# Scatters of the first static block earlier, scaling of the second ahead of the next lists' sum, in a routed two-layer MLP behind pooled attention

## The chip, the cores and the metric

One core of one Trainium2 chip runs the whole program. The metric is device microseconds of one execution; lower is better. Engines are named as in the profile: PE is TensorE, DVE is VectorE, ACT is ScalarE, POOL is GpSimd, SP is SyncE (it only issues DMAs here).

## What is computed

Attention over pooled keys and values (8 batches, 8 heads, 576 positions, 72 pooled groups) gives 4608 rows of 512 numbers. Each row is routed to one of 8 experts, by the largest logit or, where a local gate says so, to the expert of the row before. The expert is a two-layer MLP with ReLU, and its result is scaled by the routing probability:

```python
for s in range(S):
    fresh_e = int(np.argmax(logits[b, s]))
    if s == 0 or local_gate[b, s] < 0.5:
        e = fresh_e
    else:
        e = prev_e if prev_e >= 0 else fresh_e
    prev_e = e
    ...
    h = np.maximum(x[b, s] @ w1[e], 0.0)
    out[b, s] = p[e] * (h @ w2[e])
```

## The kernel before

**Stages.** The first stage computes attention and routing for four pairs of batches and writes the rows to `x_rows` in DRAM. For each expert a list of its rows (row number and probability) is built in DRAM (`ids`) by POOL's scatters. The second stage works through the lists in blocks of 256 rows, two halves of 128. A block is: read its list entries, gather its rows by an indirect DMA from POOL, transpose them on PE, split them into a high and a low part (`x`), layer 1, layer 2, scale by the probability, scatter to `out` by an indirect DMA from POOL.

**One block on PE.** Layer 1 (`l1_mms`, L307 to L312) makes 8 slices of the hidden layer, each of 4 pairs of matmuls (L309 with 512 columns, L311 with 256) into a PSUM buffer `hp`. For each slice ACT copies a part out (L316), DVE adds the other (L317), ACT applies ReLU (L321) and DVE takes the low part (L322). From the second static block on, six PSUM buffers are in turn (three `hp`, two `tp`, one `rt`). Layer 2 (`l2`, L333) makes 24 matmuls for each half into `o_ps[h]`. Half 1 comes first, then the transposes of the rows of the next block (L277), then half 0.

**Static and dynamic blocks.** The first two blocks (numbered 0 and 1 here by "first and second static block") take the rows of the most frequent expert, and overlap with the end of attention; block number 2 (the "third block") is the first whose place in the lists comes from a table `tab` that DVE computes. It runs ahead of the loop as `two_halves` and `rest(1)`; all later ones run in a loop. `rest` scales and scatters the results of its block.

**Order.** In this stretch nothing is reordered by a scheduler: `PLAN`, `PLAN_B` and `PLAN_C` are lists of steps, carried out in that order by `do` (L731), and each engine gets its instructions in the order in which the steps issue them. An engine that waits holds all that it has behind. The steps around the change:

- `es:1`, `es:0` (L840): ACT scales the first static block's `o_ps` into `ob[:, h]`.
- `so:0`, `so:1` (L843): POOL scatters `ob[:, h]` to `out`, with row numbers `idr`. A scatter waits for the landing of the one before it.
- `fd.p:18`, `i1`, `g1` (L268): the last attention rows on POOL; list and gather (into `qt`) for the third block. `Y0`, `Y1`: its transposes and splits.
- `i2`, `i3` (L290): SP loads the list of the fourth and of the fifth block into the one tile `idp`, by 8 small DMAs each; `f1` (`ids_sum`, L297 and L294): DVE sums the four parts into `m_c` and converts the row numbers into `idk`. `i3` has to wait until `f1` has read `idp`.
- `f2` (L302): POOL gathers the fourth block's rows (into `vt_in`) by `idk`.
- `ma`, `f0`: DVE copies probabilities and row numbers of the second and third block to `m_a`, `m_i`, `m_b`.
- `M2:8` to `M2:15`: layer 2 of the second static block, half 0. Half 1 was done by `L2:16` to `L2:23`.
- `e1`: `emit_scale(1)` (DVE, L1046) scales the second static block's half 1 into `ob[:, 1]`, which the scatter `so:1` must have left; `emit_rows(1)` (POOL, L1055 to L1057) scatters it. At L1138 to L1140 the same for half 0, with `seen_o(1)` (POOL, L1049) between, which waits until the scatter of half 1 has landed.
- `ld:0`: SP loads the first changed expert's weights (4 MB) into `raw`; the first block that changes expert reads them.

Of the kernel before, what the change touches and what calls it, by code (L numbers as in the profile page):

```python
# [93 lines left out]
rV:3 L2:0 s:0 rP:3 fd.p:19 h0:7 s:0 L1:8 s:0 p2.d:2 L2:1 h1:6 L1:9 L2:2 ct:0 L2:3 L2:4 L2:5 s:0 h1:7 p2.d:3 h0:8 h0:9  # L94
L2:6 L2:7 tc:0 cn:0 s:0 L2:8 L2:9 s:0 s:0 s:0 h1:8 L1:10 L2:10 L1:11 h1:9 s:0 tb:0 h0:10 L1:12 s:0 h0:11 s:0 s:0 L2:11
tb:0 h1:10 L2:12 s:0 L1:13 L2:13 s:0 tb:0 tb:0 tb:0 s:0 s:0 es:1 h0:12 L1:14 L2:14 tb:0 h1:11 L2:15 s:0 es:0 L1:15
fd.p:18 L2:16 tb:0 i1:0 L2:17 g1:0 h0:13 tb:0 L2:18 h1:12 h1:13 h0:14 L2:19 L2:20 h0:15 h1:14 L2:21 h1:15 L2:22 L2:23
Y0:0 i2:0 Y1:0 f1:0 ma:0 i3:0 f2:0 so:0 so:1 f0:0
""")
PLAN_C = plan("""  # L100
ld:0 M2:8 M2:9 M2:10 M2:11 e1:0 M2:12 M2:13 M2:14 M2:15
""")

@with_exitstack
def moe_attention(ctx: ExitStack, tc: tile.TileContext, q, q_st, k, v, v_st, w_gate, w1, w2, out):
# [231 lines left out]
    with ExitStack() as actx:  # L337
# [393 lines left out]
        def do(name, n):  # L731
# [5 lines left out]
            elif op == "lk":  # L737
                kg[n] = prep_k(n // 2, n % 2)
                step(kg[n])
            elif op == "lv":  # L740
                vg[n] = prep_v(n // 3, n % 3)
                step(vg[n])
            elif op == "lc":
                late_consts()
            elif op == "pf":
                prefill()
            elif op == "ci":
                fill()
            elif op == "cm":
                mask_consts()  # L750
            elif op == "cr":
                route_consts()
            elif op == "cz":
                nc.gpsimd.memset(kdz[n], 0.0)
            elif op == "wa":
                warm()
            elif op in ("kp", "kc"):
                step(kg[n])
            elif op == "vm":
                place_v(n // 3, n % 3)  # L760
            elif op in ("vp", "vt", "vc", "vl", "vd"):
                step(vg[n])
            elif op == "sc":
                sc[n] = scores(qT.pop(n), *units[n])
                step(sc[n])
            elif op in ("mx", "sb"):
                step(sc[n])
            elif op == "ex":
                att[n] = Attend(step(sc[n]), *units[n])
            elif op in ("T0", "T1", "T2"):  # L770
                tr2[n, op] = att[n].transpose(int(op[1]))
                step(tr2[n, op])
            elif op in ("T0c", "T1c", "T2c"):
                drain(tr2[n, op[0:2]])
            elif op in ("v0", "v1", "v2"):
                vl[n, op] = att[n].values(int(op[1]))
                step(vl[n, op])
            elif op in ("v0c", "v1c", "v2c"):
                drain(vl[n, op[0:2]])
            elif op == "fr":  # L780
                pr = units[n][0]
                if pr not in lgs:
                    lgs[pr] = ap2.tile([P, NC, GL], F32, name="lg")
                fr[n] = att[n].scale(lgs[pr])
                step(fr[n])
            elif op == "fs":
                drain(fr[n])
            elif op == "fp":
                rw[n] = att[n].rows()
                step(rw[n])  # L790
            elif op == "fd":
                drain(rw[n])
            elif op == "rA":
                fin[n] = finish(lgs[n], n)
                step(fin[n])
            elif op in RSTEPS:
                step(fin[n])
            elif op == "s":
                scatter()
            elif op == "ch":  # L800
                choose()
            elif op == "er":
                reg["e"] = number(est_i[0:1, 0:1], (EN.SP,), E - 1)
                reg["row"] = number(est_i[0:1, 1:2], (EN.SP,), (E - 1) * REG // 32)
                reg["next"] = number(est_i[0:1, 2:3], (EN.SP,), (E - 1) * REG // 32 + NS * TB)
            elif op == "w1":
                first1[n] = ld.tile([P, F], F32, name="kt", bufs=2)
                load1(first1.get, reg["e"], [n])
            elif op == "w2":
                first2[n] = ld.tile([P, 2, D], F32, name="vt_in", bufs=3)  # L810
                load2(lambda c: first2[c].rearrange("p k n -> p (k n)"), reg["e"], [n])
            elif op == "p1":
                split1(first1[n], n, nc.vector if arg else nc.gpsimd)
            elif op == "p2":
                split2(first2[n], n, nc.vector if arg else nc.gpsimd)
            elif op == "il":
                rows_load(bass.ds(reg["row"] + n * TB, TB) if n else bass.ds(reg["row"], TB), n)
            elif op == "ga":
                xgs[n] = ld.tile([P, 2, D], F32, name="qt", bufs=4)
                rows_gather(n, xgs[n], 4 * S)  # L820
            elif op in ("X0", "X1"):
                xtp[n, op] = rows_turn(int(op[1]), xgs[n])
            elif op in ("X0c", "X1c"):
                if n not in xts:
                    xts[n] = (sp if n else ld).tile([P, KD, 2, 2 * P], F32R, name="x2", bufs=1)
                rows_split(int(op[1]), xtp[n, op[0:2]], xts[n])
            elif op == "ma":
                rows_meta(m_a, NS - 1)
                nc.vector.tensor_copy(out=m_i, in_=idrs[NS - 1])
            elif op == "L1":  # L830
                l1_mms(hp[n % 3], n % KF, xts[n // KF])
            elif op == "h0":
                l1_h(hp[n % 3], n % KF)
            elif op == "h1":
                l1_l(n % KF)
            elif op == "L2":
                l2(1 - n % 16 // KF, [n % KF])
            elif op == "es":
                h = n % 2
                nc.scalar.activation(out=ob[:, h, :], in_=o_ps[h], func=AF.Copy, scale=idms[n // 2][:, h, 1:2])  # L840
            elif op == "so":
                h = n % 2
                nc.gpsimd.indirect_dma_start(out=outv, out_offset=bass.IndirectOffsetOnAxis(ap=idrs[n // 2][:, h:h + 1], axis=0),  # L843
                                             in_=ob[:, h, :], in_offset=None, bounds_check=NT - 1, oob_is_err=False)
            elif op == "M2":
                l2(1 - n // KF, [n % KF])
            elif op == "tc":
                table_consts()
            elif op == "tb":
                step(tg)  # L850
            elif op == "ct":
                acc = state["acc"]
                reg["ct"] = ps_t.tile([P, 512], F32, name="tp")
                nc.tensor.matmul(out=reg["ct"][:, 0:E], lhsT=ones, rhs=acc, start=True, stop=True)
            elif op == "cn":
                nc.vector.tensor_scalar(out=nots2, in0=isf, scalar1=done[:, 0:1], scalar2=None, op0=ALU.mult)
                nc.vector.tensor_tensor(out=cnt, in0=reg["ct"][:, 0:E], in1=nots2, op=ALU.subtract)
                nc.vector.scalar_tensor_tensor(out=cnt, in0=isf, scalar=float(2 * P + 1), in1=cnt, op0=ALU.mult, op1=ALU.max)
            elif op == "i1":
                rows_load(bass.ds(reg["next"], TB), NS)  # L860
            elif op == "g1":
                xgs["n"] = ld.tile([P, 2, D], F32, name="qt", bufs=4)
                rows_gather(NS, xgs["n"])
            elif op in ("Y0", "Y1"):
                xt = xts[NS - 1]
                xtp["n", op] = rows_turn(int(op[1]), xgs["n"])
                rows_split(int(op[1]), xtp["n", op], xt)
            elif op == "i2":
                ids_load(bass.ds(entry(2, 1, (EN.SP,), NU32 - TB), TB))
            elif op == "ld":  # L870
                n0 = entry(0, 3, (EN.SP,), E - 1)
                load1(rw1, n0)
                load2(rl2, n0)
            elif op == "e1":
                emit_scale(1)
                emit_rows(1)
            elif op == "f0":
                rows_meta(m_b, NS)
            elif op == "f1":
                ids_sum()  # L880
            elif op == "f2":
                xg = ld.tile([P, 2, D], F32, name="vt_in", bufs=3)
                gather()
            elif op == "i3":
                ids_load(bass.ds(entry(3, 1, (EN.SP,), NU32 - TB), TB))
            else:
                raise ValueError(name)
# [247 lines left out]
        l2(1)  # L1135
        turn_next()

    emit_scale(0)  # L1138
    seen_o(1)
    emit_rows(0)  # L1140
    hp += [ps_t.tile([P, 512], F32, name="tp") for _ in range(2)] + [ps_r.tile([P, 512], F32, name="rt")]
    two_halves()
    chg, nx = changes(1)
# [55 lines left out]
```

## Time and profile before

| | us |
|---|---|
| runs (3) | 648.17, 649.9, 650.04; median 649.9 |
| profiled execution | 654.89 |
| its span, first to last instruction | 653.2 |
| PE busy in it | 610.4 (93%) |
| DVE, ACT, POOL busy | 397.9, 289.6, 279.0 |
| mean granted clock of PE | 0.976 of full speed |

All durations below come from the profiled execution, which took 5.0 us more than the median of the runs. A timeline row gives the start, the duration of one (or of xN merged), the engine, the line, the operation with the tile that it writes and those that it reads (buffer numbers left out), and, in brackets, how long the engine was idle before it and what ended that. Starts are us from the first instruction. A matmul's row is longer than the step to the next one, since matmuls overlap.

### The profile page before, as it was taken

The page shows a single profiled execution, that of the slowest core. Times are in us where ns is not written, and L with a number is a line of the kernel's source. Part 1 is how long each engine was busy: PE and PEld are TensorE (multiplying, and loading weights), DVE is VectorE, ACT ScalarE, POOL GpSimd, SP SyncE. Part 2 cuts the span into 40 slices and gives each one's busy share as a digit, 9 for nine tenths or more (in the row PEclk, how much of TensorE's full clock was granted, in tenths as well). Part 3 has the DMA queues.
Part 4 walks back from the last instruction along what each step waited for, and adds up shares of the span by engine and source line. Part 5 has one row for each costly group of instructions (what it writes and reads, how often), then busy time and mean ns, then how long its engine had stood idle before and what let it go on. Part 6 is the DMA issues. An engine that isn't in the chain of part 4 may idle for free. (4 is left out here: it accounts for less than half of the span.)

```text
span 653.2 us, 14583 instructions
## 1 busy us (share of the span) xinstructions
PE 610.4 (93%) x3492; PEld 526.1 (81%) x3493; DVE 397.9 (61%) x964; ACT 289.6 (44%) x692; POOL 279.0 (43%) x480
## 2 busy tenths in 40 slices
PE   5999999989999499999999999999999996999991
PEld 4998988878877478888888888888888885888881
DVE  6998898898754143533672574778253578444350
ACT  3777767855422122331642363755132555233230
POOL 4896766854651233223043333335332155213312
PEclk9999999989999889999999999999999997999996
DMA  8998976834011742022272156457311077302101
GB/s 318 377 377 277 371 285 180 277 100 178 18 33 34 249 140 59 22 65 65 84 238 65 43 161 193 156 194 242 120 41 53 26 260 264 117 27 65 49 16 52
DMA packets 55112, 96.21 MB, mean 147 GB/s; under 512 B 30762, under 2 KB 30762, under 8 KB 55084
## 3 DMA queue, kind: packets, MB, share of 16 engines
q1 hardware_dynamic: 46572, 73.81, 33.8%
q0 software_dynamic: 8512, 22.07, 10.4%
q8 instruction: 13, 0.21, 0.1%
q14 instruction: 15, 0.12, 0.1%
HBM read 75.74 MB, written 22.21 MB: 150 GB/s over the span
## 5 line engine op out<-in xcount | busy, mean ns | idle before, releaser
L309 PE MATMUL hp<-x,w1h 128*128 128x512 f32 x364 | 135.2, 410 | 14.4 <-DVE hs L317 9.2
L333 PE MATMUL o_ps<-w2h,ht_h 128*128 128x512 f32 x312 | 124.0, 398 | 0.0
L333 PE MATMUL o_ps<-w2l,ht_h 128*128 128x512 f32 x312 | 122.1, 391 | 0.8 <-DVE w2l L176 0.7
L311 PE MATMUL hp<-x,w1l 128*128 128x256 f32 x364 | 103.9, 285 | 0.0
L309 PEld LDWEIGHTS hp<-x,w1h 128*128 128x128 f32 x364 | 70.6, 194 | 34.1 <-DVE hs L317 10.3
L333 PE MATMUL o_ps<-w2h,ht_l 128*128 128x512 f32 x312 | 87.6, 390 | 0.0
L316 ACT COPY hs<-hp 128x256 f32<-128x256 f32 x91 | 33.5, 370 | 119.6 <-PE hp L311 109.6
L321 ACT ACTIVATE ht_h<-hs 128x256 fp32r<-128x256 f32 x136 | 57.1, 420 | 40.1 <-DVE hs L317 29.0
L1046 DVE TENSOR_SCALAR ob<-o_ps,m_a 128x512 f32<-128x512 f32 x42 | 31.4, 750 | 67.8 <-PE o_ps L333 41.5
L311 PEld LDWEIGHTS hp<-x,w1l 128*128 128x128 f32 x364 | 70.9, 195 | 0.5
L333 PEld LDWEIGHTS o_ps<-w2l,ht_h 128*128 128x128 f32 x312 | 58.8, 188 | 12.4 <-DVE w2l L176 1.7
L333 PEld LDWEIGHTS o_ps<-w2h,ht_l 128*128 128x128 f32 x312 | 58.6, 188 | 12.5
L333 PEld LDWEIGHTS o_ps<-w2h,ht_h 128*128 128x128 f32 x312 | 58.8, 188 | 11.9
L538 PE MATMUL op<-vaug,aT 128*128 128x148 f32 (+4 forms) x448 | 65.6, 305 | 0.6 <-ACT osb L354 0.5
L317 DVE TENSOR_TENSOR hs<-hp,hs 128x256 f32<-128x256 f32 x91 | 37.6, 421 | 45.9 <-ACT hs L316 41.4
L1066 POOL TENSOR_TENSOR vt_in<-idk,zf 128x2 f32<-128x2 f32 x20 | 3.9, 195 | 143.1 <-PE tp L277 70.0
L538 PEld LDWEIGHTS op<-vaug,aT 128*128 128x128 f32 (+1 forms) x448 | 60.0, 178 | 3.9 <-issue 1.3
L322 DVE SCALAR_TENSOR_TENSOR ht_l<-hs,ht_h 128x256 fp32r<-128x256 f32 x136 | 56.6, 418 | 5.9 <-ACT ht_h L321 4.8
L1057 POOL DMA_INDIRECT out<-ob,m_e x42 | 47.9, 1142 | 20.9 <-issue 20.9
L302 POOL DMA_INDIRECT vt_in<-x_rows,idk x42 | 45.4, 1080 | 23.7 <-issue 12.9
L284 ACT CAST x<-tp 128x512 fp32r<-128x512 f32 x46 | 24.8, 587 | 55.7 <-PE tp L277 53.5
L1049 POOL TENSOR_TENSOR ob<-zf 128x1 f32<-128x1 f32 x41 | 9.1, 223 | 93.3 <-DMA out<-ob,m_e 83.3
(251 smaller groups left out, 1168.9 us busy)
## 6 DMA issues: line engine op xcount, KB each, us to landing
raw<-in_moe_w SPq DMA_DIRECT2D x56, 512.0 KB
kk<-in_k SPq DMA_DIRECT2D x16, 576.0 KB
qt<-in_q SPq DMA_DIRECT2D x16, 512.0 KB
vt_in<-in_v SPq DMA_DIRECT2D x16, 512.0 KB
x_rows<-xs SPq DMA_DIRECT2D x16, 512.0 KB
idp<-ids SPq DMA_DIRECT2D x176, 1.0 KB
vt_in<-in_v_st SPq DMA_DIRECT2D x8, 256.0 KB
vt_in<-in_moe_w SPq DMA_DIRECT2D x4, 512.0 KB
```

What stands on the lines that cost most here:

```text
L284: nc.scalar.copy(out=xt[:, cs, 0, :], in_=tv)
L302: nc.gpsimd.indirect_dma_start(out=xg[:, h, :], out_offset=None, in_=x_rows[0:NT + 1], in_offset=bass.IndirectOffsetOnAxis(ap=idk[:, h:h + ...
L309: nc.tensor.matmul(out=ps, lhsT=W1[0][:, kk, f * P:(f + 1) * P], rhs=xt[:, kk].rearrange("p i n -> p (i n)"), start=(kk == 0), stop=False, ...
L311: nc.tensor.matmul(out=ps[:, 0:2 * P], lhsT=W1[1][:, kk, f * P:(f + 1) * P], rhs=xt[:, kk, 0, :], start=False, stop=(kk == KD - 1), skip_g ...
L316: nc.scalar.copy(out=hb[:, 0, :], in_=ps[:, 2 * P:])
L317: nc.vector.tensor_tensor(out=hb[:, 1, :], in0=ps[:, 0:2 * P], in1=hb[:, 0, :], op=ALU.add)
L321: nc.scalar.activation(out=ht[0][:, f, :], in_=hb, func=AF.Relu)
L322: nc.vector.scalar_tensor_tensor(out=ht[1][:, f, :], in0=hb, scalar=0.0, in1=ht[0][:, f, :].bitcast(F32), op0=ALU.max, op1=ALU.subtract)
L333: nc.tensor.matmul(out=to[h], lhsT=ht[i][:, kk, h * P:(h + 1) * P], rhs=W2[j][:, kk, :], start=(n == 0), stop=(n == 3 * KF - 1))
L538: nc.tensor.matmul(out=out, lhsT=lhs, rhs=rhs if len(out.shape) == 3 else rhs.rearrange("p s x -> p (s x)"), start=all(x[0] != n for x in ...
L1046: nc.vector.tensor_scalar(out=ob[:, h, :], in0=o_ps[h], scalar1=m_a[:, h, 1:2], scalar2=None, op0=ALU.mult)
L1057: nc.gpsimd.indirect_dma_start(out=outv, out_offset=bass.IndirectOffsetOnAxis(ap=m_e[h][:, 0:1], axis=0), in_=ob[:, h, :], in_offset=None, ...
```

## The change

The scatters `so:1` and `so:0` move from the end of `PLAN_B` to ahead of the gather `g1`, half 1 first. The scaling and scatter of the second static block (`e1`, and a new step `e0` in place of L1138 to L1140) move ahead of `f1`, `i3` and `f2`, and with them the last matmuls of its layer 2 (`M2:8` to `M2:15`), which stand ahead of `e0`.

```diff
@@ PLAN_B, PLAN_C
-fd.p:18 L2:16 tb:0 i1:0 L2:17 g1:0 h0:13 tb:0 L2:18 h1:12 h1:13 h0:14 L2:19 L2:20 h0:15 h1:14 L2:21 h1:15 L2:22 L2:23
-Y0:0 i2:0 Y1:0 f1:0 ma:0 i3:0 f2:0 so:0 so:1 f0:0
+fd.p:18 so:1 L2:16 tb:0 i1:0 L2:17 so:0 g1:0 h0:13 tb:0 L2:18 h1:12 h1:13 h0:14 L2:19 L2:20 h0:15 h1:14 L2:21 h1:15 L2:22
+L2:23 Y0:0 i2:0 Y1:0 ma:0 f0:0 e1:0 M2:8 M2:9 M2:10 M2:11 M2:12 M2:13 M2:14 M2:15 e0:0 f1:0 i3:0 f2:0
 """)
 PLAN_C = plan("""
-ld:0 M2:8 M2:9 M2:10 M2:11 e1:0 M2:12 M2:13 M2:14 M2:15
+ld:0
 """)
@@ do
-            elif op == "e1":
-                emit_scale(1)
-                emit_rows(1)
+            elif op in ("e0", "e1"):
+                h = int(op[1])
+                emit_scale(h)
+                if not h:
+                    seen_o(1)
+                emit_rows(h)
@@ ahead of the loop
-    emit_scale(0)
-    seen_o(1)
-    emit_rows(0)
     hp += [ps_t.tile([P, 512], F32, name="tp") for _ in range(2)] + [ps_r.tile([P, 512], F32, name="rt")]
     two_halves()
```

In the changed kernel the lines behind `do`'s branch stand 3 higher in number (L1046 becomes L1049), and those behind the removed calls are back at their old numbers. The order of PE's, ACT's and SP's instructions is the same in both. On VectorE, from the split of the third block's rows (L285) to layer 1 of that block (L317), the order before was (`o_ps_2327` is half 1, `o_ps_2326` half 0):

```order
L285 TENSOR_TENSOR x_2488<-tp,x_2488 128x2x256 x2
L297 TENSOR_REDUCE m_c<-idp 128x4
L294 TENSOR_SCALAR idk<-m_c 128x2
L271 COPY m_a<-idm_129 128x4
L829 COPY m_i<-idr_132 128x2
L271 COPY m_b<-idm_130 128x4
L1046 TENSOR_SCALAR ob<-o_ps_2327,m_a 128x512
L1046 TENSOR_SCALAR ob<-o_ps_2326,m_a 128x512
L317 TENSOR_TENSOR hs<-hp_2323,hs 128x256
```

and now:

```order
L285 TENSOR_TENSOR x_2488<-tp,x_2488 128x2x256 x2
L271 COPY m_a<-idm_129 128x4
L829 COPY m_i<-idr_132 128x2
L271 COPY m_b<-idm_130 128x4
L1049 TENSOR_SCALAR ob<-o_ps_2327,m_a 128x512
L1049 TENSOR_SCALAR ob<-o_ps_2326,m_a 128x512
L297 TENSOR_REDUCE m_c<-idp 128x4
L294 TENSOR_SCALAR idk<-m_c 128x2
L317 TENSOR_TENSOR hs<-hp_2323,hs 128x256
```

The sum of the lists (L297, L294) has moved behind both scalings. On POOL, behind the last list scatter (L675), the order before was:

```order
L576 TENSOR_TENSOR xs<-osb,rr 128x512
L268 DMA qt<-x_rows,idr_133 128x512 x2
L302 DMA vt_in<-x_rows,idk 128x512 x2
L843 DMA out<-ob,idr_131 4608x512 x2
L1055 TENSOR_TENSOR m_e_2311<-m_i,zi 128x1
L1056 TENSOR_TENSOR zf_2316<-m_e_2311,ob 128x1
L1057 DMA out<-ob,m_e_2311 4608x512
L1049 TENSOR_TENSOR ob<-zf_2314 128x1
L1055 TENSOR_TENSOR m_e_2310<-m_i,zi 128x1
L1056 TENSOR_TENSOR zf_2316<-m_e_2310,ob 128x1
L1057 DMA out<-ob,m_e_2310 4608x512
```

and now:

```order
L576 TENSOR_TENSOR xs<-osb,rr 128x512
L843 DMA out<-ob,idr_131 4608x512 x2
L268 DMA qt<-x_rows,idr_133 128x512 x2
L1058 TENSOR_TENSOR m_e_2311<-m_i,zi 128x1
L1059 TENSOR_TENSOR zf_2316<-m_e_2311,ob 128x1
L1060 DMA out<-ob,m_e_2311 4608x512
L1052 TENSOR_TENSOR ob<-zf_2314 128x1
L1058 TENSOR_TENSOR m_e_2310<-m_i,zi 128x1
L1059 TENSOR_TENSOR zf_2316<-m_e_2310,ob 128x1
L1060 DMA out<-ob,m_e_2310 4608x512
L302 DMA vt_in<-x_rows,idk 128x512 x2
```

The two scatters of the first static block (L843) have moved ahead of the third block's gathers (L268), and the fourth block's gathers (L302) behind both scatters of the second static block.

## Rows read from the trace of the kernel before

**Rows 1.** The page, busy tenths in 40 slices of 16.3 us; PEclk is the granted clock.

```profile
PE   5999999989999499999999999999999996999991
...
PEclk9999999989999889999999999999999997999996
```

**Rows 2.** Waits, 185 to 245 us: waiter, releaser, us in total, times, longest.

```profile
DVE ob L1046 <- DMA out<-ob,idr: 13.4, 1, 13.4
...
PE hp L309 <- DVE hs L317: 9.2, 2, 8.5
```

**Rows 3.** Timeline of DVE (VectorE), 204 to 226 us.

```profile
204.81 1.29 DVE L285 TENSOR_TENSOR x<-tp,x 128x512 fp32r<-128x512 f32 x2 [2.99 <-ACT x L284]
211.18 0.18 DVE L297 TENSOR_REDUCE m_c<-idp 128x4 f32<-128x16 f32 x1 [5.08 <-DMA idp<-ids]
...
225.21 1.41 DVE L1046 TENSOR_SCALAR ob<-o_ps,m_a 128x512 f32<-128x512 f32 x2 [13.43 <-DMA out<-ob,idr]
```

**Rows 4.** Timeline of ACT (ScalarE), 191 to 196 us.

```profile
191.66 0.68 ACT L840 ACTIVATE ob<-o_ps,idm 128x512 f32<-128x512 f32 x1
...
195.14 0.69 ACT L840 ACTIVATE ob<-o_ps,idm 128x512 f32<-128x512 f32 x1 [2.23 <-PE o_ps L333]
```

**Rows 5.** Timeline of POOL (GpSimd), 198 to 228 us.

```profile
198.67 1.01 POOL L268 DMA_INDIRECT qt<-x_rows,idr  x1 [8.04 <-DVE idr L259]
...
211.83 0.94 POOL L302 DMA_INDIRECT vt_in<-x_rows,idk  x1 [10.76 <-DVE m_b L271]
...
214.34 1.03 POOL L843 DMA_INDIRECT out<-ob,idr  x1 [0.31 <-issue]
218.93 1.00 POOL L843 DMA_INDIRECT out<-ob,idr  x1 [3.57 <-DMA out<-ob,idr]
...
226.90 1.00 POOL L1057 DMA_INDIRECT out<-ob,m_e  x1 [0.61 <-issue]
```

**Rows 6.** Timeline of PE, 203 to 233 us: start, duration, operation, [idle before, releaser].

```profile
203.61 0.98 PE L277 MATMUL tp<-ident,qt 128*128 128x128 f32 x7 [0.56 <-DMA qt<-x_rows,idr]
...
209.90 0.39 PE L309 MATMUL hp<-x,w1h 128*128 128x512 f32 x1
...
218.25 0.28 PE L311 MATMUL rt<-x,w1l 128*128 128x256 f32 x1
227.00 0.80 PE L309 MATMUL hp<-x,w1h 128*128 128x512 f32 x1 [8.46 <-DVE hs L317]
...
232.29 0.54 PE L333 MATMUL o_ps<-w2h,ht_h 128*128 128x512 f32 x1
```

**Rows 7.** Windows: stretch, us, busy by engine (instructions), PEclk, DMA share, GB/s.

```profile
222.00:223.00 1.00, 0.00 (x0) 0.00 (x0) 0.00 (x0) 0.00 (x0) 0.00 (x0) 0.68 0.97 352
232.00:233.00 1.00, 1.00 (x5) 0.83 (x4) 0.17 (x2) 0.42 (x2) 0.00 (x0) 0.70 0.20 74
```

**Rows 8.** Line 1057, the scatters of the dynamic blocks: start of issue to landing.

```profile
DMA to landing us min/median/max: 2.3/2.8/7.4
```

**Rows 9.** Timeline of PE, a later block of 256 rows.

```profile
281.09 0.39 PE L309 MATMUL hp<-x,w1h 128*128 128x512 f32 x1
...
292.38 0.40 PE L333 MATMUL o_ps<-w2h,ht_h 128*128 128x512 f32 x1
...
304.22 0.39 PE L309 MATMUL hp<-x,w1h 128*128 128x512 f32 x1
```

**Rows 10.** Timeline of SP's queue, 203 to 221 us.

```profile
203.57 13.97 SPq L290 DMA_DIRECT2D idp<-ids  x16
218.76 1.96 SPq L163 DMA_DIRECT2D raw<-in_moe_w  x4
```

**Rows 11.** Line 170, first reads of the loaded weights: durations in ns, first and last start.

```profile
L170 ACT CAST w1h<-raw x24: 1037/1047/1053, 318.4 to 538.9; 128x1024 fp32r<-128x1024 f32 x24
```

**Rows 12.** Windows, columns as in group 7.

```profile
199.00:200.00 1.00, 1.00 (x6) 0.85 (x5) 1.00 (x9) 0.71 (x3) 0.70 (x2) 1.00 0.00 0
214.00:215.00 1.00, 1.00 (x7) 0.89 (x6) 0.00 (x0) 0.00 (x0) 0.69 (x2) 1.00 0.66 211
```

## The prediction

> **What bounds the kernel now.** I read the page's slices first [rows 1]: TensorE (PE) is at 9 tenths nearly everywhere, so time is to be had only where it dips. It dips to 4 in slice 14 (212 to 229 us), and the granted clock falls in slices 14 and 15. The longest waits of the stretch [rows 2] name the chain: VectorE (DVE) held its scaling of `ob` for 13.4 us until the DMA `out<-ob,idr` had landed, and PE's layer-1 matmul waited for VectorE's next sum in `hs`, 9.2 us in two waits. The timelines show it in order. VectorE reads the new lists at 211.18 (after 5.08 us of waiting for `idp`) and then starts nothing until 225.21, when both scalings run [rows 3]. They overwrite `ob`, which holds the first static block's rows; ScalarE had filled it by 192.34 and 195.83 [rows 4], yet POOL scatters these rows only at 214.34 and 218.93, behind four gathers, and the second scatter starts 3.57 us after the first, whose landing it waits for [rows 5]. PE fills its six result buffers and stops after 218.25; it resumes at 227.00, 8.46 us idle [rows 6]. The clock of PE passes from its 2.4 GHz level to 1.2 GHz within 222 to 223 and returns within 232 to 233 [rows 7], so the last two of the eight slices run at half speed.
>
> **What the change does, and the sum.** It adds and removes no computation; it moves POOL and VectorE steps.
>
> *The two scatters, to ahead of the gather for the third block.* The VectorE wait that they ended was 13.4 us [rows 2]. Now the first can be issued right after 192.34. An issue takes 1.03 us [rows 5], and such a scatter lands 2.3 to 2.8 us after its start in the shortest and median case, 7.4 in the longest [rows 8]. So the first lands about 195.2; the second needs ScalarE's 195.83 as well, starts about 196.0, ends its issue about 197.1 and lands by 198.8. At 206.1, when VectorE has split the last rows [rows 3], `ob` is free: that wait goes whole.
>
> *What it is worth is read from PE, not from VectorE's 13.4 us.* Layer 1 of an undisturbed block, the same 64 matmuls in the same shapes, takes 292.38 − 281.09 = 11.29 us [rows 9]. Begun at 209.90 it ends at 221.19, where in the trace it ends at 232.29 [rows 6]: **11.10 us**, 8.46 of waiting and 2.6 of half clock. Layer 2 of this block ran at the high clock from 233 on; I count nothing there. The Trainium skill, "TensorE: Matmul & The Clock Gate" (Part 1, What's actually happening), puts the ramp penalty at under 1% of a typical span for modelling and advises against fitting a count of slow matmuls: by that the sum would leave the 2.6 us out and end near 641.4. The trace agrees with the size (0.4%), but it is a quarter of this gain, so the rows' sum counts it.
>
> *The scalings, to ahead of the lists' sum.* The first needs layer 2's first half, done before 203; it runs about 206.4 to 207.1. The second needs PE's last matmul before 209.90 plus its drain, and ends about 210.9. The lists come in at 211.18 as before, so their sum is not later. The queue behind it on VectorE is the sum of slice 0, which can't start before about 211.9 anyway. Cover: PE has six slices of buffers and stops only at 218.25, so lists up to 6 us late would cost nothing. I cost this at 0; without that cover it would cost each microsecond in full.
>
> *The gather for the third block, now behind the scatters on POOL.* Before, it started at 198.67, when VectorE had its row numbers [rows 5]; the second scatter's issue ends 197.1, so 0 is my value. PE already waits 0.56 us for this gather [rows 6], so any delay counts in full. Upper bound: both scatters take 7.4 us; the second starts at 200.4, the gather at 201.7, 3.0 us late. A gain here is excluded: row numbers and rows come when they did. I take 0.1, nearest to the median landing.
>
> *The next gather (`vt_in`), now behind two scatters of the second block.* A scatter starts 0.94 us after its scaling (225.96 to 226.90) [rows 3, 5], so about 208.1; POOL waits for its landing (210.9 in the median case), issues the second at about 211.9 and the gathers at 213.2 and 214.5, against 211.83 before. They land about 217.3. PE transposes them after layer 1 and half of layer 2: 221.19 + 5.5 = 226.7 (half of 304.22 − 292.38, less the transposes) [rows 9]. Worst case, every landing 7.4 us: 208.1 + 7.4 + 0.9 + 1.3 + 1.3 + 7.4 = 226.4. Still in time: 0 to 0.5, I take 0.
>
> *SP's queue is passed by nothing, but its waits are.* Its second set of list loads waits for the sum on VectorE; that stays at 211.4, so the loads of the next expert start at 218.76 as before [rows 10]. Nobody reads them until 318.4 [rows 11], 88 us of cover after the last is issued. After this block everything is PE's own sequence, at 9 tenths to the end but for one stall that hangs on its own block (slice 34) [rows 1], so the gain arrives at the end.
>
> Sum: −11.10 + 0.1 = −11.0 us. The profiled execution took 654.89 us (span 653.2), which would become 643.9; it is 5.0 us above the median of the runs, 649.9, so on the runs I forecast 649.9 − 11.0 = **638.9 us**.
>
> **The rivals.**
> *A. The wait moves to the third block's gather.* The scatters stand ahead of it, in the stretch in which VectorE is densest (199 to 200: busy 1.00 [rows 12]), and land late. For it: POOL waits in order, and PE already waits for this gather. Against it: the gather's issue at 198.67 took 1.01 us under that VectorE load, the scatter's at 214.34 1.03 us with VectorE idle [rows 5, 12], so issuing isn't slowed there; and DMA is idle at 199 [rows 12]. Price by the bound above up to 3.0 us: 640 to 642. The Trainium skill, "SBUF — State Buffer" (SBUF: two separate sides, with its part on the bandwidth-pool intuition), says that a VectorE operation in a two-port mode locks GpSimd out and starves the descriptors of its DMAs; it gives some 620 ns alone against 3100 ns beside a copy, by which I estimate 2.5 us more for each scatter. That would put the time at about 642; the two issues above speak against it.
>
> *B. No change.* VectorE would have to stay blocked. The second scaling waits for the second scatter; for the old stall it would have to land after 225. Even at 7.4 us each it lands at 207.8, before PE's result at 210 lets the scaling run. Time 649.9.
>
> *C. Slower: the gather into `vt_in` meets the weight loads.* It now leaves nearer to 218.76, and the hardware queue then carries 4 MB. If it stood behind all of them (the clock row of 232 to 233 shows DMA share falling to 0.20 there [rows 7]) and took 7.4 us more, it would land at 239.4: PE would wait 12.7 us at 226.7 and lose 2.6 to the clock again, 15.3 against 11.1 gained: 654.1 us. It decides from a landing after about 235.2; the longest landing in the trace would have to be nearly three times as long. For it: the longest landings are those under loads, and the scatter issued at 218.93 held VectorE until 225.21. Against it: its issue ends over 3 us before the loads begin.
>
> **How the numbers follow.** Forecast 0.85, A 0.08, B 0.03, C 0.04. A measurement of this kernel can tell about 0.3%, 2 us. Forecast and A are faster by more: 0.93; B is the same: 0.03; C slower: 0.04. The range goes from the lowest run less the full gain, 648.17 − 11.3 = 636.9, rounded to 636.5, to A's bound of 641.9 with the runs' scatter, 642.5.
>
> **What would show it.** PE's layer 1 of the second static block without idle time and at clock 1.00, ending near 221.2; the scatters `out<-ob,idr` on POOL at about 192.7 and 196.0; the scaling rows of VectorE at about 206.4 and 210.1, the second ended by PE and not by a DMA; `qt` gathered at 198.7 and PE's wait for it still about 0.6 us; `vt_in` gathered near 213.2 with no wait of PE at its transposes. The prediction is wrong if PE idles over a microsecond anywhere between 203 and 235, if the clock falls there, or if the end moves by less than the second block does.

## The result, and the profile after

| | before | changed |
|---|---|---|
| median of the runs beside each other, us | 649.75 | 640.06 |
| runs, us | 648.17 to 650.04 (4) | 638.51 to 641.49 (4) |
| ratio of the runs, 95% interval | | 0.9855 [0.9826, 0.9885] |
| profiled execution, us (its span) | 654.89 (653.2) | 639.39 (637.5) |
| mean granted clock | 0.976 | 0.984 |

By the ratio the changed kernel is faster by 9.4 us (7.5 to 11.3 by the interval; the two medians differ by 9.7), and its median lies in the predicted range of 636.5 to 642.5. The same kernel, run twice more beside the experiments, gave 0.9821 [0.9799, 0.9843] in one group and 0.9847 [0.9822, 0.9871] in the other. The forecast, 638.9 of 649.9, is a ratio of 0.9831 and lies in all three.

The slices of the page, PE's busy tenths and granted clock. PE's 4 in slice 14 and the clock's 8s in slices 14 and 15 [rows 1] are gone:

```profile
PE   5999999989999999999999999999999987999991
...
PEclk9899999999999999999999999999999997999996
```

The two profiles differ by 15.5 us, more than the runs do. So I compare stretches, not totals. PE in the changed kernel (start, duration, operation, [idle before, releaser]):

```profile
198.13 1.07 PE L277 MATMUL tp<-ident,qt 128*128 128x128 f32 x5
...
204.84 0.39 PE L309 MATMUL hp<-x,w1h 128*128 128x512 f32 x1
...
216.13 0.40 PE L333 MATMUL o_ps<-w2h,ht_h 128*128 128x512 f32 x1
...
229.09 0.47 PE L933 MATMUL hp<-w1h,x 128*128 128x512 f32 x1 [0.97 <-DVEq L1148]
```

Layer 1 of the second static block now takes 216.13 − 204.84 = 11.29 us without an idle row, where it took 22.39 [rows 6]. It begins 5.07 us earlier than before. Of that, 0.42 us are the eight transposes of the third block's rows, which took 1.15 us after 1.57; the rest was there before them. I don't put it down to the change: over the ten profiles of this study the time from the first transposes of routed rows (about 150 us) to this layer is 55.5 to 58.2 us in the five with the scatters ahead of the third block's gather, and 55.2 to 58.3 us in the five with them behind it. From the start of this layer to layer 1 of the next 256-row block, half block included, it was 257.89 − 209.90 = 47.99 us and is now 241.86 − 204.84 = 37.02: **10.97 us gained here**. At the start of that layer PE is 16.0 us ahead of its old times, and from there to the end it stays 15.6 to 16.2 us ahead, so about 0.4 us of it is lost later.

VectorE in the changed kernel, the rows that answer to [rows 3]:

```profile
201.16 0.74 DVE L1049 TENSOR_SCALAR ob<-o_ps,m_a 128x512 f32<-128x512 f32 x1
205.04 0.75 DVE L1049 TENSOR_SCALAR ob<-o_ps,m_a 128x512 f32<-128x512 f32 x1 [3.14 <-PE o_ps L333]
205.90 0.18 DVE L297 TENSOR_REDUCE m_c<-idp 128x4 f32<-128x16 f32 x1
```

Neither scaling waits for a landing any more; the second waits for PE, and the lists' sum behind it finds `idp` there already. POOL, the rows that answer to [rows 5]:

```profile
187.46 1.02 POOL L843 DMA_INDIRECT out<-ob,idr  x1 [0.17 <-issue]
192.43 0.99 POOL L843 DMA_INDIRECT out<-ob,idr  x1 [3.95 <-ACT hs L316]
193.73 0.98 POOL L268 DMA_INDIRECT qt<-x_rows,idr  x1 [0.30 <-DVE rowf L1036]
...
202.88 1.02 POOL L1060 DMA_INDIRECT out<-ob,m_e  x1 [0.65 <-issue]
205.81 0.18 POOL L1052 TENSOR_TENSOR ob<-zf 128x1 f32<-128x1 f32 x1 [1.91 <-DMA out<-ob,m_e]
...
206.97 1.02 POOL L1060 DMA_INDIRECT out<-ob,m_e  x1 [0.57 <-issue]
208.30 1.00 POOL L302 DMA_INDIRECT vt_in<-x_rows,idk  x1 [0.30 <-issue]
```

All four scatters are issued by 208, before SP issues the weight loads at 213.14. PE's granted clock is 1.00 over the whole of 195 to 240 us. The window in which it fell before [rows 7], which in this profile lies at the half block's transposes, now reads (us, busy by engine, clock, DMA share, GB/s):

```profile
222.00:223.00 1.00, 1.00 (x10) 0.91 (x8) 0.70 (x2) 0.73 (x2) 0.20 (x1) 1.00 1.11 447
```

### The profile page after: what moved, and what is told of

The parts are those of the page before. It is cut to its first block, busy times and chain, and to the rows that moved or that the text cites. A ratio compares the mean times of both kernels' runs of the same rounds, so it can differ in the third digit from the quotient of the medians.

```text
span 637.5 us, 14589 instructions
## 1 busy us (share of the span) xinstructions
PE 606.4 (95%) x3492; PEld 524.5 (82%) x3493; DVE 398.5 (63%) x964; ACT 289.9 (45%) x692; POOL 278.4 (44%) x480
## 5 line engine op out<-in xcount | busy, mean ns | idle before, releaser
L309 PE MATMUL hp<-x,w1h 128*128 128x512 f32 x364 | 133.0, 405 | 5.4 <-DVE x L285 5.2
L333 PEld LDWEIGHTS o_ps<-w2l,ht_h 128*128 128x128 f32 x312 | 58.7, 188 | 10.8
L1049 DVE TENSOR_SCALAR ob<-o_ps,m_a 128x512 f32<-128x512 f32 x42 | 31.5, 749 | 56.9 <-PE o_ps L333 52.6
L317 DVE TENSOR_TENSOR hs<-hp,hs 128x256 f32<-128x256 f32 x91 | 37.8, 421 | 46.3 <-ACT hs L316 45.1
L302 POOL DMA_INDIRECT vt_in<-x_rows,idk x42 | 45.4, 1081 | 13.1 <-issue 9.9
L284 ACT CAST x<-tp 128x512 fp32r<-128x512 f32 x46 | 24.8, 587 | 55.5 <-PE tp L277 53.3
```

The lines of the kernel that those rows point to most:

```text
L284: nc.scalar.copy(out=xt[:, cs, 0, :], in_=tv)
L302: nc.gpsimd.indirect_dma_start(out=xg[:, h, :], out_offset=None, in_=x_rows[0:NT + 1], in_offset=bass.IndirectOffsetOnAxis(ap=idk[:, h:h + ...
L309: nc.tensor.matmul(out=ps, lhsT=W1[0][:, kk, f * P:(f + 1) * P], rhs=xt[:, kk].rearrange("p i n -> p (i n)"), start=(kk == 0), stop=False, ...
L317: nc.vector.tensor_tensor(out=hb[:, 1, :], in0=ps[:, 0:2 * P], in1=hb[:, 0, :], op=ALU.add)
L333: nc.tensor.matmul(out=to[h], lhsT=ht[i][:, kk, h * P:(h + 1) * P], rhs=W2[j][:, kk, :], start=(n == 0), stop=(n == 3 * KF - 1))
L1049: nc.vector.tensor_scalar(out=ob[:, h, :], in0=o_ps[h], scalar1=m_a[:, h, 1:2], scalar2=None, op0=ALU.mult)
```

## The experiments

Eight runs, of six further kernels and of the change twice, in two groups on one chip. In the first group, of four, the kernel before took 650.11 us, in the second 654.48; so each run is compared with the kernel before of its own group. "L1 to L1" is the stretch named above, from layer 1 of the second static block to layer 1 of the next 256-row block: 47.99 us before, 37.02 in the change.

### Which half of the change does it?

The kernel before with the two scatters moved, and nothing else:

```diff
-fd.p:18 L2:16 tb:0 i1:0 L2:17 g1:0 h0:13 ...
+fd.p:18 so:1 L2:16 tb:0 i1:0 L2:17 so:0 g1:0 h0:13 ...
-Y0:0 i2:0 Y1:0 f1:0 ma:0 i3:0 f2:0 so:0 so:1 f0:0
+Y0:0 i2:0 Y1:0 f1:0 ma:0 i3:0 f2:0 f0:0
```

> The change's first part alone: the two scatters of the first static block ahead of the third block's gather; the lists' sum stays ahead of the scalings. Theory (the wait for the scatters' landing was the whole loss, the order of sum and scalings is worth nothing): VectorE reads the lists at about 211, scales right after until about 213, PE has no idle time in layer 1 of the second static block, and the ratio to before is that of the change, 0.983 to 0.986. Rival (the scalings' move brings a share of its own): VectorE or PE still waits at least 2 us there, ratio 0.989 or more.

Measured: 638.63 us, ratio 0.9836 [0.9811, 0.9861]; layer 1 in 219.20 − 207.91 = 11.29 us, L1 to L1 37.20. The change, run beside it:

> The change itself, unaltered, timed against before in five rounds. Theory (11.0 us in the second static block, nothing else): ratio 0.983 (0.981 to 0.985), and layer 1 of the second static block takes 11.3 us on PE in this profile too. Rival (the change costs something elsewhere, or the profile's earlier start of that block belongs to it): ratio 0.985 or more with 11.3 us in layer 1, or a start of the block near 205 us again where before has 210.

Measured: 638.5 us, ratio 0.9821 [0.9799, 0.9843], layer 1 in 11.29 us, L1 to L1 37.10. One sign named for the rival did come: the block starts at 203.77 us. But it starts at 203.94 in a kernel below whose scatters stand behind the third block's gather, so an early start doesn't come with the change. The two intervals overlap, and the stretch of 37.20 us lies within 0.2 us of the change's (37.02, 37.10, and 37.20 in its third profile): the scatters carry the whole gain, and the earlier scaling adds nothing that can be measured. VectorE of the kernel with the scatters alone:

```profile
208.63 0.18 DVE L297 TENSOR_REDUCE m_c<-idp 128x4 f32<-128x16 f32 x1 [4.54 <-DMA idp<-ids]
...
209.14 1.40 DVE L1046 TENSOR_SCALAR ob<-o_ps,m_a 128x512 f32<-128x512 f32 x2
```

The scalings still stand behind the lists, and are done at 210.5, soon enough for slice 0. What the earlier scaling buys is slack on POOL, as that queue shows in the same kernel:

```profile
217.40 1.01 POOL L1057 DMA_INDIRECT out<-ob,m_e  x1 [0.57 <-issue]
225.45 0.18 POOL L1049 TENSOR_TENSOR ob<-zf 128x1 f32<-128x1 f32 x1 [7.03 <-DMA out<-ob,m_e]
225.83 0.20 POOL L1066 TENSOR_TENSOR vt_in<-idk,zf 128x2 f32<-128x2 f32 x1 [0.20 <-PE tp L277]
```

Here the block's last scatter is issued after SP has begun the weight loads (215.87) and seen landed 8.05 us after its start; POOL is just in time for the next fetch, which PE's transposes release at 225.6. In the changed kernel's first profile POOL has seen that landing at 210.59 and then waits for PE:

```profile
210.59 0.20 POOL L1052 TENSOR_TENSOR ob<-zf 128x1 f32<-128x1 f32 x1
222.75 0.20 POOL L1069 TENSOR_TENSOR vt_in<-idk,zf 128x2 f32<-128x2 f32 x1 [11.96 <-PE tp L277]
```

### Ahead of which gather must the scatters stand?

The kernel before with the scatters moved past one gather only (`f2`), still behind the one for the third block (`g1`):

```diff
-Y0:0 i2:0 Y1:0 f1:0 ma:0 i3:0 f2:0 so:0 so:1 f0:0
+Y0:0 i2:0 Y1:0 f1:0 ma:0 i3:0 so:0 so:1 f2:0 f0:0
```

> Before, but with the two scatters moved only past the fourth block's gather (vt_in), which waits for the lists; they stay behind the third block's gather (qt). Theory (the loss came from standing behind a gather that waits for lists): the scatters start at about 201.4 and 204.5, land by 208.8, VectorE scales from 211.8 on without a wait for them, ratio as the change, 0.983 to 0.986. Rival (they must stand ahead of the third block's gather to land in time): VectorE waits for them past 214 and PE loses at least 2 us, ratio 0.988 or more. Should placing them ahead of the third block's gather cost anything, this one is faster than the change.

Measured: 639.48 us, ratio 0.9845 [0.9825, 0.9866]; layer 1 in 11.29 us, L1 to L1 37.57. The scatters start 8.5 us ahead of layer 1, as said, and 3.2 us ahead of it, 2.2 us later than said, since the first takes longer to land; VectorE has no wait for either. POOL:

```profile
195.44 1.03 POOL L843 DMA_INDIRECT out<-ob,idr  x1 [0.30 <-ACT ht_h L321]
200.73 1.00 POOL L843 DMA_INDIRECT out<-ob,idr  x1 [4.26 <-DMA out<-ob,idr]
206.22 0.99 POOL L302 DMA_INDIRECT vt_in<-x_rows,idk  x1 [4.49 <-DVE m_b L271]
```

POOL waits for the lists at the third row, as it did before, for 10.76 us [rows 5]; only now the scatters have left ahead of that wait. Two steps swapped in a list give the gain of the whole change, as far as the intervals tell; L1 to L1 is 0.4 to 0.6 us longer than in the change's profiles. The loss of the kernel before was that ready scatters stood behind a gather that couldn't start.

### Is it the buffer, or the landing?

The kernel before, its scatters late as they were, but with the first static block's rows in a buffer of their own, so that VectorE has no landing to wait for:

```diff
-nc.scalar.activation(out=ob[:, h, :], in_=o_ps[h], ...
+ob1 = ld.tile([P, F], F32, name="kt", bufs=2).rearrange("p (h d) -> p h d", h=2)
+nc.scalar.activation(out=ob1[:, h, :], in_=o_ps[h], ...
...
-    in_=ob[:, h, :], in_offset=None, bounds_check=NT - 1, oob_is_err=False)
+    in_=ob1[:, h, :], in_offset=None, bounds_check=NT - 1, oob_is_err=False)
```

> Before, but the first static block's rows go to a buffer of their own, so that the scalings of the second overwrite nothing; the scatters stay late. Theory (it is the buffer that makes VectorE wait): the 13.4 us wait of VectorE goes, layer 1 takes 11.3 us, though the scatters still land only at about 225. The late landing then holds POOL's scatters of the second block into the next stage (it copies the row numbers that VectorE wants to overwrite at about 224), so PE loses 2 to 4 us again at the block's end: ratio 0.986 to 0.990. Rival (it is not the buffer but POOL's or the DMA queue's order that holds VectorE): VectorE waits as before, ratio 0.998 to 1.002.

Measured: 651.4 us, ratio 1.001 [0.999, 1.003]: the expectation failed. Yet the stall is gone: layer 1 took 218.23 − 206.94 = 11.29 us. Everything came back one block later: L1 to L1 is 256.24 − 206.94 = 49.30 us, more than before. POOL, VectorE and PE of this kernel:

```profile
211.49 1.03 POOL L845 DMA_INDIRECT out<-kt,idr  x1 [0.30 <-issue]
217.32 1.00 POOL L845 DMA_INDIRECT out<-kt,idr  x1 [4.81 <-DMA out<-kt,idr]
225.31 1.00 POOL L1059 DMA_INDIRECT out<-ob,m_e  x1 [6.49 <-DMA out<-kt,idr]
231.99 0.18 POOL L1051 TENSOR_TENSOR ob<-zf 128x1 f32<-128x1 f32 x1 [5.68 <-DMA out<-ob,m_e]
...
237.05 1.00 POOL L302 DMA_INDIRECT vt_in<-x_rows,idk  x1 [0.25 <-issue]
```

```profile
232.35 0.17 DVE L294 TENSOR_SCALAR m_i<-m_b 128x2 int32<-128x2 f32 x1 [11.26 <-POOL m_e L1057]
...
236.37 0.75 DVE L1048 TENSOR_SCALAR ob<-o_ps,m_a 128x512 f32<-128x512 f32 x1 [1.18 <-POOL ob L1051]
```

```profile
236.96 0.77 PE L932 MATMUL hp<-w1h,x 128*128 128x512 f32 x1 [6.73 <-DVEq L1150]
247.90 1.94 PE L277 MATMUL tp<-ident,vt_in 128*128 128x128 f32 x8 [2.95 <-remote]
```

Four scatters, each waiting for the landing of the one before it, fill POOL from 211 to 236, most of it beside the weight loads. The next fetch leaves at 237.05, where the kernel with the scatters alone sends it at 226.44. VectorE is held by POOL, PE by VectorE for 6.73 us, and then PE waits another 2.95 us. The profile calls what ended that second wait "remote"; I read it as the fetched rows, because in four kernels with this wait (this one, the two delays, the splits first) it ends 9.3 to 9.6 us after the second gather's start, wherever that lies (in the swap, where the wait is only 0.24 us, 10.8). The expectation had the first hold right in kind, but priced it at 2 to 4 us and left out the next fetch. So here the late scatters cost as much with a second buffer as without: the reuse of `ob` was only the first place where they were waited for.

### How much cover is there?

The kernel with the swap, and a delay on POOL ahead of the scatters: `n` fills of an otherwise unused tile.

```diff
-... ma:0 i3:0 so:0 so:1 f2:0 f0:0
+... ma:0 i3:0 dz:12 so:0 so:1 f2:0 f0:0
+elif op == "dz":
+    for _ in range(n):
+        nc.gpsimd.memset(pad, 0.0)
```

> The run that moves the scatters only past the fourth block's gather, with 12 memsets of 128x512 (about 0.5 us each, 6 us) on POOL ahead of them; the memsets fill a tile that nobody reads. Theory (PE loses nothing as long as the scatters land by the time at which its six buffers are full, about 8.5 us after the start of layer 1, less the two scalings): they land about 5.5 us after its start, VectorE waits for them, PE does not; the second scatter of the second block then falls into the weight loads, and VectorE may wait 1 to 2 us for POOL at the block's end, still without PE: ratio 0.983 to 0.987. Rival (every microsecond of later landing is a microsecond of time): ratio 0.991 or more.

Measured: 644.1 us, ratio 0.9846 [0.9818, 0.9874]; the full gain. POOL, then VectorE:

```profile
203.75 6.96 POOL L879 MEMSET pad<- 128x512 f32 x12
210.97 1.03 POOL L843 DMA_INDIRECT out<-ob,idr  x1 [0.27 <-issue]
214.03 1.00 POOL L843 DMA_INDIRECT out<-ob,idr  x1 [2.03 <-DMA out<-ob,idr]
```

```profile
217.11 1.41 DVE L1050 TENSOR_SCALAR ob<-o_ps,m_a 128x512 f32<-128x512 f32 x2 [2.50 <-DMA out<-ob,idr]
```

VectorE waits 2.50 us for the landing, and PE's layer 1 still takes 223.84 − 212.55 = 11.29 us: the six result buffers are the cover, as the prediction had it. (The expectation had no wait of PE at the block's end; there is one, 1.78 us at the half block's transposes, and L1 to L1 is 38.75.) With 18 fills (`dz:18`):

> The same with 18 memsets, 9 us. Theory: the second scatter starts about 5.5 us after the start of layer 1 and lands at 8.5 to 12; PE stops at 8.5 and resumes at 12 to 15, 3.5 to 6.5 us idle, with up to 2.6 us of low clock behind it, and VectorE waits again for POOL's copy of the row numbers at the block's end: ratio 0.989 to 0.998. Rival (the cover is larger than the six buffers): as the run with 6 us. Rival (the landing has no cover): 0.996 or more already with 6 us, and over 1.000 here.

Measured: 654.2 us, ratio 0.9989 [0.9971, 1.0007]: more lost than expected, nearly all of the gain. The fills took 10.45 us. VectorE, PE, and the two scatters behind them:

```profile
217.61 1.41 DVE L1050 TENSOR_SCALAR ob<-o_ps,m_a 128x512 f32<-128x512 f32 x2 [6.24 <-DMA out<-ob,idr]
...
235.65 0.75 DVE L1050 TENSOR_SCALAR ob<-o_ps,m_a 128x512 f32<-128x512 f32 x1 [5.07 <-POOL ob L1053]
```

```profile
219.40 0.51 PE L309 MATMUL hp<-x,w1h 128*128 128x512 f32 x1 [1.24 <-DVE hs L317]
...
246.90 1.10 PE L277 MATMUL tp<-ident,vt_in 128*128 128x128 f32 x8 [2.90 <-remote]
```

```profile
219.33 1.02 POOL L1061 DMA_INDIRECT out<-ob,m_e  x1 [0.64 <-issue]
227.36 0.19 POOL L1053 TENSOR_TENSOR ob<-zf 128x1 f32<-128x1 f32 x1 [7.01 <-DMA out<-ob,m_e]
...
235.43 0.18 POOL L1053 TENSOR_TENSOR ob<-zf 128x1 f32<-128x1 f32 x1 [5.89 <-DMA out<-ob,m_e]
```

In the block itself the buffers gave out, as foreseen, but PE was idle for 1.24 us and not 3.5 to 6.5: VectorE went on 8.08 us after the start of layer 1, at the early end of the landing that was expected. Layer 1 took 12.80 us. The expectation missed the size of what follows: the second block's scatters now start at 219.33, after SP has begun the weight loads (218.02), are seen landed 8.03 and 6.90 us after their start (228.53 for the second), and the next fetch leaves at 236.32. L1 to L1 is 45.79 us, 8.77 more than in the change: 1.24 + (1.91 − 0.97) + 2.90 = 5.1 us of PE's waits, and by difference some 3.7 us, most of which lies in two stretches at half clock (0.50 in 238 to 241 and in 248 to 251).

### A version that might beat the change

One stall of the page is left, in slice 34: layer 1 of the block that changes expert waits 5.05 us for the split of its rows, which stands behind other VectorE work. PE in the changed kernel:

```profile
529.18 0.76 PE L309 MATMUL hp<-x,w1h 128*128 128x512 f32 x1 [5.05 <-DVE x L285]
```

The change, with the splits first in `rest`:

```diff
 def rest(j, chg, nx):
+    for c2 in range(2):
+        rows_split(c2, hp[3 + c2], xt)
     meta_shift()
     ids_sum()
...
     emit_rows(1)
-    for c2 in range(2):
-        rows_split(c2, hp[3 + c2], xt)
     l2(0)
```

> The change, and in every dynamic block the splits of the next block's rows moved on VectorE ahead of the numbers, the lists' sum and the first scaling. Theory (after the change the largest wait of PE left is the one at the change of weights behind a half block, 5.05 us, where the splits stand behind 2.4 us of these steps): that wait shrinks to 2.5 to 3 us, no other block waits, 2 to 3 us faster than the change, ratio 0.978 to 0.981. Rival (the later fetch, lists and scalings of the ordinary blocks cost PE as much): no faster than the change.

> The change itself once more, on the chip of the three other runs, to be compared with them. Theory: ratio 0.981 to 0.985, and 24.3 us from the start of layer 1 of the second static block to the start of the third block, against 35.2 before. Rival: as in the first repeat.

Measured: the change 643.97 us, ratio 0.9847 [0.9822, 0.9871], 24.40 us from layer 1 to the third block; with the splits first 648.02, ratio 0.9904 [0.9873, 0.9936], so 4 us slower. The stall did shrink, to 2.65 us as expected, but new ones came, on PE:

```profile
240.93 1.08 PE L277 MATMUL tp<-ident,vt_in 128*128 128x128 f32 x8 [1.80 <-remote]
...
535.22 0.47 PE L309 MATMUL hp<-x,w1h 128*128 128x512 f32 x1 [2.65 <-DVE x L285]
```

Two more half blocks wait 1.1 us each for their rows. At the last block's half 0 of layer 2 PE is only 1.49 us behind the change's profile (623.64 against 622.15), and 0.74 of that was there at layer 1 of the second static block. The greater part comes after it: the last fetch leaves later, and both last scatters stand behind it on POOL. The fetch needs the row numbers `idk`, which now stand behind the splits on VectorE; at this place that is read from the order of steps, but at 229.41 of the same run the profile names VectorE's `idk` as what POOL waited for. First the change, then the splits first:

```profile
623.25 1.01 POOL L302 DMA_INDIRECT vt_in<-x_rows,idk  x1 [0.30 <-issue]
...
630.37 1.02 POOL L1060 DMA_INDIRECT out<-ob,m_e  x1 [0.57 <-issue]
```

```profile
628.13 1.00 POOL L302 DMA_INDIRECT vt_in<-x_rows,idk  x1 [0.32 <-issue]
...
635.41 1.02 POOL L1060 DMA_INDIRECT out<-ob,m_e  x1 [0.57 <-issue]
```

The last scatter leaves 5.04 us later, as much as the two profiles differ (647.76 − 642.67 = 5.1). No kernel of this study beats the change by more than its interval.

## Why the prediction was right

Times of the changed kernel are set on the time scale of the profile before by adding 5.07 us; "on the old scale" below means that.

- **The sum's main term, 11.10 us in layer 1: right.** 22.39 − 11.29 = 11.10, no idle row, clock 1.00. Its two parts were read from rows, and the half clock's 2.6 us is confirmed at another place: the stall that remains takes 5.05 us before 529.18, and its layer 1 then takes 543.11 − 529.18 = 13.93 us, 2.64 over 11.29. The Trainium skill's rule ("TensorE: Matmul & The Clock Gate", Part 1, What's actually happening), by which the sum would leave this out, gives 641.4, a ratio of 0.9869: two of the three intervals hold that (up to 0.9885 and 0.9871), one doesn't (up to 0.9843). The runs leave it open; the profile shows the 2.6 us in full.
- **The scalings' move, 0: right.** The scatters alone give the same stretch within 0.2 us. The named times held: 206.4 and 210.1 were said, 206.23 and 210.11 measured, the second ended by PE.
- **The cover of six slices: right in the block, too simple behind it.** A delay of 7 us left layer 1 at 11.29 us, one of 10 us cost it 1.51, of which 1.24 were waiting. But "after this block everything is PE's own sequence" isn't safe by itself. It holds in the change, whose scatters are all issued ahead of the weight loads. With the second block's last scatter issued behind them, PE lost nothing (scatters alone), 0.24 (the swap) or 1.78 us (7 us delay) at the half block's transposes. With both of that block's scatters behind them, the second buffer and the longer delay paid 12.3 and 7.3 us (L1 to L1 less layer 1, against the change) one block later, through POOL's chain of scatters and the fetch behind it. The prediction looked for a late fetch in one place, the gather into `vt_in` of this block (rival C); it comes one fetch further on.
- **The gather for the third block, +0.1: no cost seen.** It left at 193.73, 198.80 on the old scale, against 198.7 foreseen. A wait of PE of about 0.6 us was said to remain: PE's matmul rows show none now, but its weight loads at these transposes still wait 0.5 us for `qt` (0.9 before). I don't put the difference down to the change: in the five profiles with the scatters ahead of this gather that wait is 0.4 to 0.7 us, in the five with them behind it anything from none (the swap, the second buffer) to 0.9. Rival A didn't come about.
- **`vt_in`: right.** Foreseen at 213.2 without a wait, gathered at 213.37, and no wait at PE's transposes.
- **The scatters' own times: off, without effect.** They left at 187.46 and 192.43, on the old scale 192.53 and 197.50, against about 192.7 and 196.0. The first agrees by luck: said to follow ScalarE at once, it stood behind POOL's list work though its rows were ready at 185.17. The second left when ScalarE was done, as said, but ScalarE was later. VectorE's scaling waited for neither.
- **SP's loads, unmoved: right.** They begin at 213.14, 218.21 on the old scale, against 218.76. Their cover was misread: from the last issue (222.7) to the first read (318.4) it is 96 us, not 88, which changes nothing.
- **Layer 2, nothing counted: right to 0.14 us** (12.82 us before, 12.96 now up to the half block; PE's wait there grew from 0.70 to 0.97). In the change's other two profiles that wait is 1.00 and 1.10 us, so the sign "PE idles over a microsecond" is touched there, by a wait that the kernel before has too.
- **The end moves by a little less than the block.** The ends of the two profiles lie 15.7 us apart, the starts of layer 1 behind the second static block 16.0. By its own words this is a sign against the prediction; it is 0.3 us, and the runs don't show where it goes.

Rival B fell with the first row of VectorE, rival C with the transposes. The runs' 9.4 us fall short of the forecast 11.0, but the interval (7.5 to 11.3) holds both, and the other two measurements of the change (11.6 and 10.0 us) stand on both sides of 11.

## What to carry to other kernels

On an engine that works in order, ask of each step that is ready what it stands behind: here ready scatters stood behind a gather that waited 10.8 us for its indices, and swapping two steps was worth as much as the whole change. A wait for a buffer may be only the first place where a late transfer is felt: before giving it a second buffer, follow who waits for that transfer next (here the next scatter, then the next fetch, then TensorE). Size the gain on the engine that bounds (11 us on TensorE), not on the longest wait in the list (13.4 us on VectorE), and try delays of two lengths to find out how much cover there is.

## What the runs showed of the hardware

- **The same stretch of program ends at different times from profile to profile.** The first transposes of routed rows, with the same instructions ahead of them in all ten profiles, started anywhere from 148.21 to 154.30 us (the change in its second profile, then the kernel with the 7 us delay). No step that was moved or added runs before that:

```profile
148.21 0.60 PE L277 MATMUL tp<-ident,qt 128*128 128x128 f32 x4
```

```profile
154.30 0.60 PE L277 MATMUL tp<-ident,qt 128*128 128x128 f32 x4
```

- **A scatter was seen landed later beside the weight loads.** POOL saw it landed 2.9 us after its start where they weren't under way (202.88 to 205.81 in the change), and 6.7 to 8.6 us after it where it was issued behind them (225.31 to 231.99 with the second buffer, 224.24 to 232.88 with the 7 us delay).
- **The clock can fall after the engine has resumed.** With the splits first, PE resumed at 535.22 after 2.65 us of idling; its granted clock was 0.95 in 535 to 536 and 0.50, its 1.2 GHz level, in 536 to 539; the layer took 547.96 − 535.22 = 12.74 us, 1.45 over the undisturbed one. I had expected a fall only within an idle stretch, as at 222 [rows 7].
